# A fused attention, expert and readout kernel: softplus in two chains, and the one-hot rows of the slots placed later in the first expert

## The chip, the cores and the metric

The kernel runs on one core of a Trainium2 chip. The metric is the device time of one launch in microseconds (us). The kernel before was timed three times: 517.79, 516.14 and 516.80 us, median 516.8 us.

## The reference

Three layers follow each other: a retention attention, a layer of 8 experts of which each token uses two, and a dense layer with a softmax-weighted unit and a layer norm.

```
for t in range(S):                                    # B=2, H=8, S=768, D=64
    state = gamma * state + k[:, :, t] (x) v[:, :, t]
    y[:, :, t] = scale * q[:, :, t] @ state
x = y as 1536 rows of 512
logits = x @ w_gate                                   # 512 x 8
noisy  = logits + log1p(exp(x @ w_noise)) * noise
top2 of each row, weights by softmax over the two
out[row] += weight * (relu(x[row] @ w1[e]) @ w2[e])   # w1 512x1024, w2 1024x512, 8 experts
h = out @ w_in; solu = h * softmax(h); ln = (solu - mean) / sqrt(var + 1e-6) * g_ln
result = ln @ w_out
```

## The kernel before, in words

**Stages.** The attention runs over 12 tiles of 128 rows (`for i in range(NT)`): scores, output, state update and a turn of the output into rows (`x_rows`), which also yields the logits of the gate and of the noise scale. The rows are stored to the DRAM tensor `xd`. While it runs, the routing is worked out in four groups of tiles (`GROUPS`: tiles 0 to 3, 4 to 7, 8 and 9, 10 and 11). Then eight experts are worked through, one after the other, and after them the dense layer, again by tiles of 128 rows.

**Number format.** The experts' matmuls take each operand as a high and a low part (`wh` and `wl` of the weights, `xh` and `xl` of the rows, `hh` and `hl` of the hidden values). ACT writes the high part as a copy, DVE the low part as a difference. A hidden group (`hidden(e, f, ...)`, line 723) is 12 matmuls into one PSUM bank: eight with `xh`, then four with `xl`. ACT (line 727) and DVE (line 728) empty it.

**Routing.** `choose(g)` computes the softplus of the noise scale with a polynomial of degree 8 in |tanh(z/2)| (line 509, seven dependent steps), the noisy logits, the top two (`top`, `chosen`) and a running count (`cum`). `rank(g)` turns `chosen` and `cum` into ranks with two small matmuls. `slots(lo, hi)` works in two halves: first the ranks of the two chosen experts of every row (lines 564 to 571), then one-hot rows `nm` and `hot` (lines 579 to 585). `add_table` multiplies `nm` with `hot` on PE and adds the result to `table`, which then tells which row stands in which slot. `by_rows` spreads it, `lists` makes from it the row numbers `rows_r` for experts 1 to 7 (line 671), and `load_xg(1)` gathers the 448 rows of expert 1 from `xd` with four indirect DMAs on POOL (line 998). Those rows are turned by PE (line 1028) inside the second half of expert 0 (`second`, line 1071).

**Expert 0 is split.** Which rows it has is known in two steps: 192 early rows from tiles 0 to 7 (`first_xt(0, ...)`) and 256 late rows (`list_part(1, ...)`, gathered and turned by `first_xt(1, ...)`, lines 634 to 639). The loop at line 971 runs the eight hidden groups f = 0 to 7 for the early rows; the loop at line 1087 runs the same eight for the late rows. Between the groups stand the routing steps, at places written out by hand with conditions on f. Everything is issued in the order in which the Python code runs (a manual schedule): each engine takes its own instructions in that order, so a step on DVE delays all that is written after it on DVE.

**Weights.** `advance(0, j)` after every second late group splits one more weight unit (lines 200 and 201) and issues later loads.

Of the kernel before, what the change touches and what calls it, by code (L numbers as in the profile page):

```python
# [8 lines left out]
F32 = mybir.dt.float32  # L9
# [6 lines left out]
AF = mybir.ActivationFunctionType  # L16
OP = mybir.AluOpType
# [5 lines left out]
LOG2 = (0.006006605044301197, -0.034264599930674204, 0.09229041734241328, -0.16499812980379158,  # L23
        0.2394333707327323, -0.331446652240305, 0.49982549864312487, -0.999993630258501,
        0.6931471414508898)
# [19 lines left out]
def retnet_moe_solu(ctx, tc, qT, kT, k, v, w_gate, w_noise, noise, w1, w2, w_in, w_out, g_ln,  # L45
                    decay, out, dbg=None):
    nc = tc.nc
# [4 lines left out]
    E = w1.shape[0]  # L52
# [229 lines left out]
    causal = const.tile([128, 128], F32, name="causal")  # L282
# [3 lines left out]

    decT = {}
    step = const.tile([128, NC, HP], F32, name="step")
    one = rt.tile([1, 128], F32, name="one", bufs=1)
    nc.gpsimd.memset(one, 1.0)  # L290

    def dec_t(c):
        if c >= NC:
# [197 lines left out]
    def choose(g):  # L491

        lo, hi = GROUPS[g]
        n_t = hi - lo
        t = rt.tile([128, 4, n_t, E], F32, tag="rt", name="rt", bufs=3)
        th, r, ab, nl = (t[:, n] for n in range(4))
        p = lgs[:, lo:hi]
        ii = slice(lo, hi)
        V = nc.vector

        nc.scalar.activation(th, p[:, :, E:2 * E], AF.Tanh, scale=0.5)
        nc.scalar.activation(r, p[:, :, E:2 * E], AF.Relu)
        yield
        V.scalar_tensor_tensor(ab, th, -1.0, th, op0=OP.mult, op1=OP.max)
        V.tensor_scalar_mul(nl, ab, LOG2[0])
        for n, c in enumerate(LOG2[1:-1]):
            if n == 2 and g == 2:
                yield
            V.scalar_tensor_tensor(nl, nl, c, ab, op0=OP.add, op1=OP.mult)
        V.scalar_tensor_tensor(nl, nl, LOG2[-1], r, op0=OP.add, op1=OP.add)  # L510
        V.tensor_mul(nl, nl, nz[:, ii, :])
        V.tensor_add(nl, nl, p[:, :, :E])
        yield
        ix = rt.tile([128, n_t, 8], U32, tag="ix", name="ix")
        for s in range(n_t):
            V.max(top[:, lo + s, :], nl[:, s])
        V.tensor_tensor(chosen[:, ii, :], nl, top[:, ii, 1:2].to_broadcast([128, n_t, E]), op=OP.is_ge)
        for i in range(lo, hi):
            V.tensor_add(cum[:, i + 1], cum[:, i], chosen[:, i])
        yield  # L520
        for s in range(n_t):
            V.max_index(ix[:, s], top[:, lo + s, :], nl[:, s])
        V.tensor_copy(top_i[:, ii, :], ix[:, :, :2])
# [447 lines left out]
    for f in range(KF):  # L971
        hidden(0, f, slice(0, EARLY), (lambda: newest(2 + f // 2)) if f in (0, 2) else None)
        if f == 3:
            list_part(1, range(4, 12), "c2", last=True)
            for p in last_picks:
                next(p, None)
            todo = slots(4, 10)
            next(todo)
        if f == 4:
            turns()  # L980
        if f == 5:
            next(todo, None)
            next(picks, None)
    for p in range(2):
        first_xt(1, 2 * p)

# [96 lines left out]
    for e in range(E - 1):  # L1083
        if e:
            hidden_of(e)
        for j in range(4):
            for f in (2 * j, 2 * j + 1):
                hidden(e, f, slice(0 if e else EARLY, CAPS[e]))
                if not e and f == 0:
                    todo = slots(10, NT)  # L1090
                    next(todo)
                if not e and f == 1:
                    next(todo, None)
                if not e and f == 3:
                    add_table(4, "c2")
                    add_table(10, "c3")
                    by_rows()
                if not e and f == 5:
                    lists()
                    for _ in load_xg(1):  # L1100
                        pass
                    rt_ctx.close()
                    gx["pool"] = gx_ctx.enter_context(tc.tile_pool(name="gx", bufs=1, side="right"))
                if e == 1 and f in (1, 3):
                    next(rows, None)
                if e and e + 2 < E and f < 4:
                    fresh = fresh if f else load_xg(e + 2)
                    nc.gpsimd.tensor_copy(pace, H_t[e][0][:1, f, :1])  # L1108
                    next(fresh)
                if e and f in (5, 7):  # L1110
                    next(fresh, None)
                if e and f in (1, 3, 4, 5):
                    d = (1, 3, 4, 5).index(f)
                    y_st = y_t(e - 1, d)
                    next(y_st, None)
                    y_bank(e, d)
                elif e:
                    convert()
                    if f == 6:
                        next(y_st, None)  # L1120
                elif not e and f > 5:
                    for d in ((0, 1), (2, 3))[f - 6]:
                        y_bank(e, d)
            advance(e, j)
            if e and j > 1:
                next(y_st, None)
# [259 lines left out]
```

## Time and profile before

| | |
|---|---|
| median of three runs | 516.8 us |
| the profiled execution: its time | 515.93 us |
| its span on the core | 513.8 us |
| PE busy | 505.3 us (98%) |
| DVE busy | 365.7 us (71%) |
| ACT, POOL busy | 232.2 us (45%), 111.2 us (22%) |
| late rows' first hidden group starts | 82.21 us |
| second half of expert 0 starts | 96.64 us |

Times of the trace are counted from the start of the span. PE is the matmul engine and PEld its weight loads; a busy PE is not a PE at its peak, since matmuls overlap and their ends are modelled. A row of the timeline has the start, the duration, the engine, the line, the operation with output and inputs, and in brackets the idle time of the engine just before it with what ended it.

### The profile page before, as it was taken

To read this page: it belongs to the slowest core of one execution; us is meant where nothing else is said; L and a number is where in the kernel's file an instruction comes from. 1 tells how busy PE (TensorE), PEld (TensorE's weight loads), DVE (VectorE), ACT (ScalarE), POOL (GpSimd) and SP (SyncE) were. 2 spreads that over 40 slices of the span, in tenths; PEclk is the share of its full clock that TensorE was granted. 3 is DMA by queue.
4 is the path that set the end of the run, shared out by engine and by line. 5 is a ranking of instruction groups with operands and counts; after the bars stand their busy time and mean duration, and the time that the engine had idled before them with its cause. 6 is when DMAs were issued, how large, how long until landed. Compare 5 with 4: busy or idle time off the path is not lost.

```text
span 513.8 us, 8621 instructions
## 1 busy us (share of the span) xinstructions
PE 505.3 (98%) x3068; PEld 462.7 (90%) x3068; DVE 365.7 (71%) x726; ACT 232.2 (45%) x436; POOL 111.2 (22%) x210
## 2 busy tenths in 40 slices
PE   9999998999999999999999999999999999999996
PEld 8898987999999999999999999998878788888885
DVE  5678778846876886787869778799187657676650
ACT  2488733643353443345335534445244634345431
POOL 4034100423003104004003000002344435431120
PEclk9999999999999999999999999999999999999999
DMA  8999531798989898989799968567553564653341
GB/s 256 308 390 355 196 99 43 236 363 250 311 251 243 283 265 214 347 214 279 262 277 305 304 169 264 183 179 202 173 175 122 145 186 141 174 160 122 102 124 47
DMA packets 71857, 111.92 MB, mean 218 GB/s; under 512 B 9760, under 2 KB 37152, under 8 KB 71808
## 3 DMA queue, kind: packets, MB, share of 16 engines
q1 hardware_dynamic: 65952, 96.54, 61.5%
q0 software_dynamic: 4368, 14.29, 9.1%
q10 hardware_dynamic: 1488, 0.48, 0.4%
q8 instruction: 26, 0.43, 0.3%
q14 instruction: 23, 0.19, 0.1%
HBM read 83.50 MB, written 27.79 MB: 217 GB/s over the span
## 4 chain that ended last, share of the span: by engine, by line
PE 80%; DVE 12%; ACT 2%; issue 2%; DMA 2%; SPq 0%; DVEq 0%; ACTq 0%
PE c L1071 21%; PE b L952 11%; PE a L723 10%; PE b L723 10%; PE d L859 10%; PE c L1193 3%; PE xr L479 3%; PE s L429 3%; PE c L446 2%; PE c L457 2%; PE c L442 2%; DVE wl L201 1%; DVE hl L728 1%; DVE yr L1052 1%; PE a L837 1%
## 5 line engine op out<-in xcount | busy, mean ns | idle before, releaser
L201 DVE TENSOR_TENSOR wl<-wr,wh 128x1024 fp32r<-128x1024 f32 x64 | 76.6, 1219 | 12.4 <-ACT wh L200 12.4
L1071 PE MATMUL c<-hh,wh 128*128 128x448 f32 (+5 forms) x224 | 79.0, 352 | 0.0
L1071 PE MATMUL c<-hh,wl 128*128 128x448 f32 (+5 forms) x224 | 78.8, 352 | 0.0
L1071 PE MATMUL c<-hl,wh 128*128 128x448 f32 (+5 forms) x224 | 78.8, 352 | 0.0
L200 ACT ACTIVATE wh<-wr 128x1024 fp32r<-128x1024 f32 x68 | 69.4, 1050 | 7.1 <-DMA wr<-in_moe_w_dram 7.0
L723 PE MATMUL b<-xh,wh 128*128 128x192 f32 (+8 forms) x144 | 47.1, 335 | 0.3 <-ACT xh L638 0.3
L723 PE MATMUL b<-xh,wl 128*128 128x192 f32 (+8 forms) x144 | 46.6, 331 | 0.0
L1071 PEld LDWEIGHTS c<-hh,wl 128*128 128x128 f32 x224 | 42.1, 188 | 1.1
L1071 PEld LDWEIGHTS c<-hl,wh 128*128 128x128 f32 x224 | 42.1, 188 | 1.1
L1071 PEld LDWEIGHTS c<-hh,wh 128*128 128x128 f32 x224 | 42.1, 188 | 1.1
L723 PE MATMUL a<-xh,wh 128*128 128x256 f32 (+7 forms) x128 | 42.9, 340 | 0.0
L723 PE MATMUL a<-xh,wl 128*128 128x256 f32 (+7 forms) x128 | 42.8, 339 | 0.0
L859 PE MATMUL d<-wh,x2h 128*128 128x512 f32 x96 | 38.8, 404 | 0.0
L1108 POOL COPY pace<-hh 1x1 f32<-1x1 f32 x20 | 9.8, 490 | 133.0 <-ACT hh L727 133.0
L952 PE MATMUL b<-wh,zh 128*128 128x512 f32 (+1 forms) x104 | 38.3, 375 | 0.0
L952 PE MATMUL b<-wl,zh 128*128 128x512 f32 (+1 forms) x104 | 38.3, 374 | 0.0
L859 PE MATMUL d<-wl,x2h 128*128 128x512 f32 x96 | 37.9, 395 | 0.0
L859 PE MATMUL d<-wh,x2l 128*128 128x512 f32 x96 | 37.8, 394 | 0.0
L727 ACT ACTIVATE hh<-b 128x192 fp32r<-128x192 f32 (+8 forms) x36 | 17.1, 476 | 44.0 <-PE b L723 42.2
L727 ACT ACTIVATE hh<-a 128x256 fp32r<-128x256 f32 (+7 forms) x32 | 15.9, 497 | 45.3 <-PE a L723 45.3
L998 POOL DMA_INDIRECT xr<-xd,rows_r x27 | 28.3, 1048 | 26.2 <-DVE rows_r L671 16.8
L1034 ACT ACTIVATE xh<-xt 128x428 fp32r<-128x428 f32 (+5 forms) x24 | 13.0, 542 | 44.8 <-DVE xt L1032 44.8
(254 smaller groups left out, 1093.4 us busy)
## 6 DMA issues: line engine op xcount, KB each, us to landing
wr<-in_moe_w_dram SPq DMA_DIRECT2D x64, 512.0 KB, 5.5
zd<-zs SPq DMA_DIRECT2D x40, 128.0 KB, 2.3
zc<-zd SPq DMA_DIRECT2D x10, 512.0 KB, 4.0
xs<-xr SPq DMA_DIRECT2D x18, 256.0 KB, 5.6
raw<-in_moe_w_in_dram SPq DMA_DIRECT2D x8, 512.0 KB, 6.4
raw<-in_moe_w_out_dram SPq DMA_DIRECT2D x8, 512.0 KB, 5.9
xq<-xs SPq DMA_DIRECT2D x16, 208.0 KB, 7.1
yg<-yr SPq DMA_DIRECT2D x16, 208.0 KB, 4.7
```

The costliest lines, as they stand in the source:

```text
L200: nc.scalar.activation(hi, t, AF.Copy)
L201: (nc.gpsimd if u < LEAD else nc.vector).tensor_sub(lo, t, hi)
L429: nc.tensor.matmul(p[:, s, hp, :], KT[i][r, hp, :], QT[i][r, hp, :], start=True, stop=True)
L479: nc.tensor.matmul(t[:, d // 2, at:at + 128 + G2], XT[i][:, d, :], unit[d // 2][:, G2 - G2 * (d % 2):][:, :128 + G2], start=(d % 2 == 0), ...
L723: nc.tensor.matmul(p, w[:, 0, f * 128:(f + 1) * 128], x[:, d, c], start=(n == 0), stop=(n == len(terms) - 1))
L727: nc.scalar.activation(hh[:, f, c], p, AF.Relu)
L859: nc.tensor.matmul(PH[i][:, s, :], x[:, c], w[:, 0, f], start=(n == 0), stop=(n == 3 * KD - 1))
L952: nc.tensor.matmul(p, z[:, f * 128:(f + 1) * 128], unit_t[8 * E + 4 + f // 2][n][:, f % 2, c], start=(m == 0), stop=(m == len(terms) - 1))
L998: nc.gpsimd.indirect_dma_start(out=t[b], out_offset=None, in_=xd[:], in_offset=bass.IndirectOffsetOnAxis(ap=rows_r[:, e - 1, b:b + 1], axi ...
L1034: nc.scalar.activation(hi, t, AF.Copy)
L1071: nc.tensor.matmul(py[d][:, :CAPS[e]], c, h[:, f, :CAPS[e]], start=(f == 0 and n == 0), stop=(f == KF - 1 and n == 2))
L1193: nc.tensor.matmul(py, h[:, f, c], w[:, f % 2], start=(f == 0 and n == 0), stop=(f == KF - 1 and n == 2))
```

## The change

Three edits are made.

1. `one`, a row of ones with a memset on POOL, is now the first row of `causal`.
2. In `choose`, ACT also computes the square of the tanh (`sq`), and the polynomial is worked out as two chains in `sq`, one for the even and one for the odd powers, which are added at the end.
3. The second half of `slots(4, 10)` and the last step of `choose(3)` leave the early loop. They stand after late groups 1 and 0. `slots(10, 12)` moves from late groups 0 and 1 to 2 and 3, the tables from 3 to 4, `lists` and the gathers of expert 1 from 5 to 6.

```diff
-    one = rt.tile([1, 128], F32, name="one", bufs=1)
-    nc.gpsimd.memset(one, 1.0)
+    one = causal[0:1, :]
...
-        t = rt.tile([128, 4, n_t, E], F32, tag="rt", name="rt", bufs=3)
-        th, r, ab, nl = (t[:, n] for n in range(4))
+        t = rt.tile([128, 5, n_t, E], F32, tag="rt", name="rt", bufs=3)
+        th, r, ab, nl, sq = (t[:, n] for n in range(5))
+        od = th
...
         nc.scalar.activation(th, p[:, :, E:2 * E], AF.Tanh, scale=0.5)
+        nc.scalar.activation(sq, th, AF.Square)
         nc.scalar.activation(r, p[:, :, E:2 * E], AF.Relu)
         yield
         V.scalar_tensor_tensor(ab, th, -1.0, th, op0=OP.mult, op1=OP.max)
-        V.tensor_scalar_mul(nl, ab, LOG2[0])
-        for n, c in enumerate(LOG2[1:-1]):
+        V.tensor_scalar_mul(nl, sq, LOG2[0])
+        V.tensor_scalar_mul(od, sq, LOG2[1])
+        for n in (2, 4, 6):
+            V.scalar_tensor_tensor(nl, nl, LOG2[n], sq, op0=OP.add, op1=OP.mult)
+            V.scalar_tensor_tensor(od, od, LOG2[n + 1], ab if n == 6 else sq, op0=OP.add, op1=OP.mult)
             if n == 2 and g == 2:
                 yield
-            V.scalar_tensor_tensor(nl, nl, c, ab, op0=OP.add, op1=OP.mult)
         V.scalar_tensor_tensor(nl, nl, LOG2[-1], r, op0=OP.add, op1=OP.add)
+        V.tensor_add(nl, nl, od)
...
         if f == 4:
             turns()
-        if f == 5:
-            next(todo, None)
-            next(picks, None)
...
                 if not e and f == 0:
+                    next(picks, None)
+                if not e and f == 1:
+                    next(todo, None)
+                if not e and f == 2:
                     todo = slots(10, NT)
                     next(todo)
-                if not e and f == 1:
+                if not e and f == 3:
                     next(todo, None)
-                if not e and f == 3:
+                if not e and f == 4:
                     add_table(4, "c2")
                     add_table(10, "c3")
                     by_rows()
-                if not e and f == 5:
+                if not e and f == 6:
                     lists()
```

**On DVE, in the softplus of the last group** (tile `rt` holds all its operands; `nz` is the noise, `lgs` the logits). Before:

```order
L504 SCALAR_TENSOR_TENSOR rt<-rt 128x16
L505 TENSOR_SCALAR rt<-rt 128x16
L509 SCALAR_TENSOR_TENSOR rt<-rt 128x16 x7
L510 SCALAR_TENSOR_TENSOR rt<-rt 128x16
L511 TENSOR_TENSOR rt<-rt,nz 128x16
L512 TENSOR_TENSOR rt<-rt,lgs 128x16
```

With the change:

```order
L506 TENSOR_SCALAR rt<-rt 128x16
L507 TENSOR_SCALAR rt<-rt 128x16
L509 SCALAR_TENSOR_TENSOR rt<-rt 128x16
L510 SCALAR_TENSOR_TENSOR rt<-rt 128x16
L509 SCALAR_TENSOR_TENSOR rt<-rt 128x16
L510 SCALAR_TENSOR_TENSOR rt<-rt 128x16
L509 SCALAR_TENSOR_TENSOR rt<-rt 128x16
L510 SCALAR_TENSOR_TENSOR rt<-rt 128x16
L513 SCALAR_TENSOR_TENSOR rt<-rt 128x16
L514 TENSOR_TENSOR rt<-rt 128x16
L515 TENSOR_TENSOR rt<-rt,nz 128x16
L516 TENSOR_TENSOR rt<-rt,lgs 128x16
```

The instructions of lines 509 and 510 belong to two chains in turn, and no instruction of one needs the one just ahead of it.

**On DVE, from the last early groups to the first late ones** (`nm` and `hot` the one-hot rows, `xl` the late rows' low parts, `hl` the hidden values' low parts, `wl` a weight unit's). Before:

```order
L728 SCALAR_TENSOR_TENSOR hl<-c_1359,hh 128x192
L579 TENSOR_TENSOR nm<-col_185,at 128x384
L582 TENSOR_TENSOR nm<-nm,number 128x384
L585 TENSOR_TENSOR hot<-col_185,at 128x1536
L522 MAX_INDEX ix<-top,rt 128x8 x2
L523 CAST top_i<-ix 128x4
L728 SCALAR_TENSOR_TENSOR hl<-b,hh 128x192
L728 SCALAR_TENSOR_TENSOR hl<-c_1397,hh 128x192
L639 TENSOR_TENSOR xl<-a,xh 128x2x256 x2
L728 SCALAR_TENSOR_TENSOR hl<-b,hh 128x256
L564 TENSOR_TENSOR eq<-e_180,top_i 128x32
```

With the change:

```order
L643 TENSOR_TENSOR xl<-a,xh 128x2x256 x2
L732 SCALAR_TENSOR_TENSOR hl<-b,hh 128x256
L526 MAX_INDEX ix<-top,rt 128x8 x2
L527 CAST top_i<-ix 128x4
L732 SCALAR_TENSOR_TENSOR hl<-a,hh 128x256
L583 TENSOR_TENSOR nm<-col_183,at 128x384
L586 TENSOR_TENSOR nm<-nm,number 128x384
L589 TENSOR_TENSOR hot<-col_183,at 128x1536
L201 TENSOR_TENSOR wl<-wr,wh 128x1024
L732 SCALAR_TENSOR_TENSOR hl<-b,hh 128x256
L568 TENSOR_TENSOR eq<-e_178,top_i 128x32
L569 TENSOR_TENSOR eq<-eq,rks 128x32
```

The six instructions of the one-hot rows and of the top-two numbers now stand behind `xl`, and the first weight unit's `wl` stands ahead of the last group's `eq`, not behind its `hot`.

**On DVE, to the row numbers of the later experts** (`spread` is the table by rows, `rows_r` the row numbers). Before:

```order
L600 TENSOR_TENSOR spread<-part_211,table 128x128
L201 TENSOR_TENSOR wl<-wr,wh 128x1024
L728 SCALAR_TENSOR_TENSOR hl<-b,hh 128x256
L728 SCALAR_TENSOR_TENSOR hl<-a,hh 128x256
L671 TENSOR_SCALAR rows_r<-c_1572 128x28
```

With the change:

```order
L604 TENSOR_TENSOR spread<-part_209,table 128x128
L732 SCALAR_TENSOR_TENSOR hl<-a,hh 128x256
L201 TENSOR_TENSOR wl<-wr,wh 128x1024
L732 SCALAR_TENSOR_TENSOR hl<-b,hh 128x256
L675 TENSOR_SCALAR rows_r<-c_1599 128x28
```

`rows_r` now follows the `hl` of late group 6, before it followed that of group 5.

## Rows read from the trace of the kernel before

**Rows 1.** The page's first part: busy time, share of the span, instructions.
```profile
PE 505.3 (98%) x3068; PEld 462.7 (90%) x3068; DVE 365.7 (71%) x726; ACT 232.2 (45%) x436; POOL 111.2 (22%) x210
```

**Rows 2.** Waits of PE, whole run: us in total, times, longest.
```profile
PE b L723 <- DVE xl L639: 1.5, 1, 1.5
```

**Rows 3.** Timeline of DVE: dependent steps of the softplus, then two independent ones.
```profile
70.18 1.43 DVE L509 SCALAR_TENSOR_TENSOR rt<-rt 128x16 f32<-128x16 f32 x7
...
78.16 0.17 DVE L570 SCALAR_TENSOR_TENSOR at<-top_i,sets 128x12 f32<-128x12 f32 x1
78.25 0.17 DVE L571 SCALAR_TENSOR_TENSOR at<-sets,ranks 128x12 f32<-128x12 int32 x1
```

**Rows 4.** Timeline of PE: first matmuls of early groups 1, 2 and 3.
```profile
69.66 0.33 PE L723 MATMUL c<-xh,wh 128*128 128x192 f32 x1
...
71.06 0.27 PE L723 MATMUL b<-xh,wh 128*128 128x192 f32 x1
...
73.14 0.33 PE L723 MATMUL c<-xh,wh 128*128 128x192 f32 x1
```

**Rows 5.** Timeline of PE's weight loads: the output of attention tile 11.
```profile
65.05 0.45 PEld L446 LDWEIGHTS c<-pm,vp 128*64 128x64 f32 x8 [0.20 <-ACT lg L484]
```

**Rows 6.** Timeline of DVE, around the late rows' low parts.
```profile
80.45 0.55 DVE L579 TENSOR_TENSOR nm<-col,at 128x384 f16<-128x384 f32 x1
...
83.17 0.08 DVE L522 MATCH_VALUE_LOAD ix<-top,rt 128x8 f32 x1
...
84.19 1.28 DVE L639 TENSOR_TENSOR xl<-a,xh 128x512 fp32r<-128x512 f32 x2
...
86.82 0.18 DVE L564 TENSOR_TENSOR eq<-e,top_i 128x32 f32<-128x32 f32 x1
...
87.91 0.42 DVE L728 SCALAR_TENSOR_TENSOR hl<-a,hh 128x256 fp32r<-128x256 f32 x1
88.25 0.28 DVE L579 TENSOR_TENSOR nm<-col,at 128x128 f16<-128x128 f32 x1
...
89.38 1.22 DVE L201 TENSOR_TENSOR wl<-wr,wh 128x1024 fp32r<-128x1024 f32 x1
90.51 0.42 DVE L728 SCALAR_TENSOR_TENSOR hl<-b,hh 128x256 fp32r<-128x256 f32 x1
```

**Rows 7.** Timeline of PE: first matmuls of late groups 0, 1, 2 and 5.
```profile
82.21 0.39 PE L723 MATMUL b<-xh,wh 128*128 128x256 f32 x1 [0.25 <-ACT xh L638]
...
85.86 0.28 PE L723 MATMUL a<-xh,wh 128*128 128x256 f32 x1
...
87.29 0.28 PE L723 MATMUL b<-xh,wh 128*128 128x256 f32 x1
...
92.10 0.28 PE L723 MATMUL a<-xh,wh 128*128 128x256 f32 x1
```

**Rows 8.** Timeline of ACT: a weight unit's high part.
```profile
94.02 1.05 ACT L200 ACTIVATE wh<-wr 128x1024 fp32r<-128x1024 f32 x1
```

**Rows 9.** Timeline of DVE: the row numbers and that unit's low part.
```profile
94.50 0.18 DVE L671 TENSOR_SCALAR rows_r<-c 128x28 uint32<-128x28 f32 x1
95.11 1.23 DVE L201 TENSOR_TENSOR wl<-wr,wh 128x1024 fp32r<-128x1024 f32 x1 [0.43 <-ACT wh L200]
```

**Rows 10.** Timeline of POOL: the fourth gather for expert 1.
```profile
98.71 1.54 POOL L998 DMA_INDIRECT xr<-xd,rows_r  x1 [0.31 <-issue]
```

**Rows 11.** Line 998, the fourth gather alone: from its start to its landing.
```profile
DMA to landing us min/median/max: 7.8/7.8/7.8
```

**Rows 12.** Line 998 from 90 to 135 us, all twelve gathers.
```profile
DMA to landing us min/median/max: 3.4/7.0/8.9
```

**Rows 13.** Timeline of PE's weight loads: expert 1's rows turned, eight blocks.
```profile
106.17 1.00 PEld L1028 LDWEIGHTS a<-unit,xr 128*128 128x128 f32 x8
```

**Rows 14.** Timeline of PE: the last matmuls of the launch.
```profile
508.27 1.07 PE L952 MATMUL b<-wh,zl 128*128 128x256 f32 x8
```

**Rows 15.** Windows: busy us and count of PE, PEld, DVE, ACT, POOL; granted clock, DMA, GB/s.
```profile
512.00:513.80 1.80, 0.00 (x0) 0.00 (x0) 0.00 (x0) 0.00 (x0) 0.00 (x0) 0.95 0.04 9
```

## The prediction

> **What bounds the kernel now.** I read the page's first part first. PE is busy for 98% of the span [rows 1], so a change can only take away, add or move waits of PE. The waits come next: over the whole run PE's longest wait for another engine is one of 1.5 us, for `xl`, the late rows' low parts, which DVE writes [rows 2]. Then come the timelines of PE and DVE from 60 to 107 us, the stretch that the change touches. There PE loses time in three places.
>
> First, the output of attention tile 11: its weight loads waited 0.20 us [rows 5]. The row names ACT, but what comes last there is DVE's masked scores, which stand behind the third group's softplus in DVE's order. Second, the last group's softplus: early group 1 of expert 0 took 71.06 - 69.66 = 1.40 us, early group 2 took 73.14 - 71.06 = 2.08 us, since `rank` behind it waits for `chosen`; 0.68 us are lost [rows 4]. Third, late group 0: it took 85.86 - 82.21 = 3.65 us where group 1 took 1.43 us [rows 7]. DVE was busy with one-hot rows from 80.45 to 83.17 us and came to `xl` only at 84.19 us [rows 6]. That loses 2.22 us. Together some 3.1 us can be won here. From 106 us on PE hardly waits, so what is won or lost up to there reaches the end.
>
> **The change, part by part.** The row of ones in place of a memset on POOL costs and gives nothing: POOL's first work lies under the loads of the start. Four more squares on ACT cost PE nothing either, because ACT is busy 45% of the span [rows 1]; were that cover gone, four instructions of some 0.2 us would be 0.8 us. No table is loaded more often in the changed order.
>
> *Two chains.* Before, 11 steps from the first product to the noisy logits depend on each other, 1.43 / 7 = 0.20 us apart. Two steps that don't depend on each other start 0.09 us apart (78.16 and 78.25) [rows 3]. With two chains the longer one has 8 steps, and the other's fit between them. That is 3 x 0.20 = 0.6 us less for the last group, nearly all of the 0.68 us that PE loses. Of the third group's second half two steps go, 0.4 us, more than the 0.20 us [rows 5]. I take 0.83 us for both places together.
>
> The Trainium skill has a rule that speaks against this part: on VectorE: DVE Perf Modes, section "The DRAIN you can't avoid", says that the next instruction doesn't start until the pipe is empty, so that independent instructions gain nothing. By it the 13 instructions in place of 12 would cost 0.2 us, not save 0.6. The pair of rows 3 speaks against it here, so I go by the pair.
>
> *`xl` first.* The one-hot rows (80.45 to 83.17, 2.72 us) and the top-two numbers leave the place ahead of `xl` [rows 6]. DVE is then free when ACT has written `xh`, and the `xl` matmuls start almost without a wait; I leave 0.1 us for that and win 2.1 us. Late group 1 would start at 85.86 - 0.83 - 2.1 = 82.93 us, group 2 at 84.36 us [rows 7].
>
> *What is late next.* The removed work now stands behind `xl` on the same engine, and PE meets it at the tables, four groups later. `hl` of group 1 starts 87.91 - 87.29 = 0.62 us behind group 2's first matmul [rows 6, 7], so at 84.98 us. From there DVE has no idle time up to the last one-hot rows: `hl` 0.34 (87.91 to 88.25), the big one-hot rows 2.72, a weight unit's `wl` 90.51 - 89.38 = 1.13, `hl` 0.34, the ranks from `eq` on 87.91 - 86.82 = 1.09, `hl` 0.34, the small one-hot rows 89.38 - 88.25 = 1.13 [rows 6]. The sum is 7.09 us, and they are written at 92.07 us. PE has finished groups 1 to 4 at 82.93 + 4 x 1.43 = 88.65 us and the larger table about 0.3 us later. It waits some 3.1 us. Group 5 then starts at about 92.25 us, against 92.10 us before [rows 7]. The wait for `xl` has become a longer wait one place later, and the balance is +0.15 us. Small errors in the seven durations and the two gains make this -0.4 to +0.6 us.
>
> *Row numbers for expert 1.* They move behind group 6, and on DVE behind its `hl` and a weight unit. ACT's split of that unit started 94.02 - 92.10 = 1.92 us after group 5 [rows 7, 8]; now 94.17 us. Its `wl` starts 95.11 - 94.02 = 1.09 us later [rows 8, 9], at 95.26, and ends at 96.39 us; `hl` takes 0.34 us more. `rows_r` starts at 96.75 us, where it was 94.50 us [rows 9]: 2.25 us later. Behind it waits POOL with the four gathers. The fourth started at 98.71 us [rows 10] and landed 7.8 us later [rows 11], at 106.51 us. PE's weight loads for the first eight turned blocks run from 106.17 us, 0.125 us apart, and the fourth block comes at 106.55 us [rows 13]. There is no slack: 0.04 us. With the change the gather starts at 100.96 us and PE asks for it at 106.70 us.
>
> How long it then takes isn't shown before, since the weight loads that share the DMA engines stay where they are. From below: 5.7 us or less hides it, and the shortest of the twelve gathers took 3.4 us. From above: 8.9 us, the longest, makes PE wait 109.86 - 106.70 = 3.15 us [rows 12]. I take the median, 7.0 us [rows 12], because this gather falls among the same loads as those that took about that long: landing at 107.96 us, a wait of 1.25 us. Nothing behind it gives that back.
>
> **Sum.** +0.15 + 1.25 = +1.4 us on the profiled execution of 515.93 us, so 517.3 us. That execution lies 0.9 us under the median of the three runs; on the median the forecast is 516.8 + 1.4 = 518.2 us. A measurement of this kernel can tell about 0.3% from no change, 1.55 us, so this counts as no change.
>
> **Rivals.**
> - *A, the forecast:* gains and the new wait for the one-hot rows cancel, and the gather lands 5.7 to 7.15 us after its start: 0 to 1.4 us of wait, time up to 518.35 us. With it the case of a hidden gather: 516.95 us. 0.52.
> - *B, slower:* the gather decides. From 7.15 us on the sum is over 1.55 us; at 8.9 us it is 0.15 + 3.15 = 3.3 us, 520.1 us. For it: the fourth gather took 7.8 us [rows 11], and would meet all of its competitors from the start. Against it: with a later start less of its own queue lies ahead of it, and the loads are further on. 0.30.
> - *C, slower, the clock:* PE stands still for 3.1 us at the tables, longer than anywhere between its first matmul and its last. After its last matmul, over at 509.34 us [rows 14], the granted clock was still nearly full: 0.95 as a mean of the last 1.8 us [rows 15], so it fell to 1.2 GHz only some 4 us after the stop. If it falls earlier here, groups 5 to 7 run at half rate: up to 3 x 1.43 = 4.3 us more, which covers the wait for the gather. With half of that, +0.15 + 2.15 = 2.3 us, 519.1 us. 0.08. The Trainium skill, TensorE: Matmul & The Clock Gate, section "HAM oscillation — how this bites in real kernels", warns of just such waits; by it the fall would come here if the wait grew a little, and no row before shows one in mid run.
> - *D, the chains bring nothing* (each DVE instruction waits for the one ahead of it): the early 0.83 us stay lost, and the one-hot rows and row numbers come 0.8 us later still, so 0.15 + 0.83 + 2.05 = 3.0 us, 519.8 us. Rows 3 speak against it. 0.04.
> - *E, faster:* DVE reaches the last one-hot rows before PE needs them, and the gather is hidden: -2.9 us, 513.9 us. DVE would have to be 3.1 us shorter on seven durations that I read from the trace. 0.06.
>
> **How the numbers follow.** The likeliest case is A: 518.2 us. The chances: faster 0.06 (E), same 0.52 (A), slower 0.42 (B, C, D). The range goes from the hidden gather less the small terms, 516.8 + 0.15 - 0.55 = 516.4 us, to just under the longest gather, 519.9 us; it leaves out E and the ends of B, C and D, less than 2 in 10.
>
> **What would show it.** Right: `xl` at about 82 us with no long wait of PE for it; `chosen` without a wait; the longest wait of PE some 3 us, at line 596, for `hot` on DVE; group 5 within half a microsecond of 92.1 us; `rows_r` near 96.7 us; a wait of PE at the turned rows near 107 us, for a DMA. Wrong: no wait at line 596 (E), a granted clock below 1.00 between 92 and 97 us (C), the steps of lines 509 and 510 spaced 0.2 us apart (D), or PE through the turned rows without a wait, in which case the time stays within half a microsecond of before.

## The result, and the profile after

The changed kernel takes 522.39 us, the median of five executions (520.20 to 523.32); the kernel before, run beside it, took 516.8 us (515.72 to 517.79). The ratio is 1.0104, with an interval of 1.0072 to 1.0136: slower by 5.6 us. The forecast was 518.2 us, and the time lies above its range (516.4 to 519.9).

The profiled execution took 521.80 us (span 519.8 us, mean granted clock 0.995) where before's took 515.93 (513.8, 1.000). Over the five executions the mean clock was 0.990 to 0.995, so all five lost some of it; only the profiled one shows where. The page's first part, against [rows 1]:

```profile
PE 506.6 (97%) x3068; PEld 464.3 (89%) x3068; DVE 365.2 (70%) x730; ACT 233.4 (45%) x440; POOL 108.9 (21%) x209
```

The engines have the same work. The two longest waits of PE over the whole run stand against the one of 1.5 us in [rows 2]:

```profile
PE a L1029 <- DMA xr<-xd,rows_r: 3.3, 2, 1.8
PE c L596 <- DVE hot L589: 3.0, 1, 3.0
```

The wait for `xl` is gone. In its place stand the tables' wait, as forecast, and two waits for gathers that have not landed (lines moved by 1 to 4). How far behind PE runs, from its first matmul of each stage:

| first matmul of | before | after | behind by |
|---|---|---|---|
| late group 0 | 82.21 | 81.65 | -0.56 |
| late group 1 | 85.86 | 83.31 | -2.55 |
| late group 5 (behind the tables) | 92.10 | 92.62 | +0.52 |
| expert 0's second part | 96.64 | 97.22 | +0.58 |
| the same, behind the first turned rows | 107.16 | 111.50 | +4.34 |
| expert 1 | 117.94 | 123.81 | +5.87 |
| end of the span | 513.8 | 519.8 | +6.0 |

So most of the loss arises in two stretches: 3.76 us at the turned rows and 1.53 us right behind them. PE's timeline there, answering to [rows 13]:

```profile
106.96 0.38 PE L1029 MATMUL a<-unit,xr 128*128 128x128 f32 x2
109.12 0.33 PE L1029 MATMUL a<-unit,xr 128*128 128x128 f32 x1 [1.79 <-DMA xr<-xd,rows_r]
110.97 0.86 PE L1029 MATMUL a<-unit,xr 128*128 128x128 f32 x5 [1.52 <-DMA xr<-xd,rows_r]
111.50 0.72 PE L1072 MATMUL c<-hh,wh 128*128 128x448 f32 x1
112.01 0.57 PE L1072 MATMUL c<-hl,wh 128*128 128x448 f32 x1
```

The third gather is waited for, then the fourth. The matmuls behind them run at half rate, as the windows show (columns as in [rows 15]):

```profile
106.00:111.40 5.40, 2.09 (x13) 1.53 (x12) 0.22 (x1) 0.06 (x1) 2.93 (x3) 1.00 1.03 377
111.40:114.60 3.20, 3.20 (x12) 2.88 (x10) 2.65 (x6) 1.96 (x3) 0.00 (x0) 0.52 1.05 404
114.60:118.00 3.40, 3.40 (x17) 3.09 (x16) 1.00 (x1) 0.00 (x0) 0.00 (x0) 0.95 0.63 152
```

After 3.3 us of standing still the granted clock is 0.52 for 3.2 us, nearly all at 1.2 GHz: 3.20 x 0.48 = 1.5 us, and 3.40 x 0.05 = 0.2 us after it, together about what the table shows for this stretch. POOL's timeline shows why the gathers are late, against [rows 10]; DVE's row of the same stretch stands under it:

```profile
97.62 0.94 POOL L999 DMA_INDIRECT xr<-xd,rows_r  x1 [20.07 <-DVE rows_r L675]
98.87 1.97 POOL L999 DMA_INDIRECT xr<-xd,rows_r  x1 [0.30 <-issue]
101.14 1.96 POOL L999 DMA_INDIRECT xr<-xd,rows_r  x1 [0.30 <-issue]
103.40 0.95 POOL L999 DMA_INDIRECT xr<-xd,rows_r  x1 [0.30 <-issue]
...
98.79 4.63 DVE L201 TENSOR_TENSOR wl<-wr,wh 128x1024 fp32r<-128x1024 f32 x4 [0.52 <-ACT wh L200]
```

The second and third gather take twice as long as the first. In the kernel before, the gathers began at 94.95 us, and three of them, of 0.95 us each, had begun when DVE's four `wl` began at 98.20 us. Now `rows_r` comes 2.67 us later, but the four `wl`, tied to ACT's splits, come only 0.59 us later (98.79), and the gathers fall among them. The fourth starts 4.69 us later than before, not 2.25. From its start to its landing it takes about as long as before (7.8 us in [rows 11]), so it lands late because it starts late:

```profile
DMA to landing us min/median/max: 7.5/7.5/7.5
```

### The profile page after: what moved, and what is told of

Same layout as the page of the kernel before. It is cut to its first block, busy times and chain, and to the rows that moved or that the text cites. A ratio compares the mean times of both kernels' runs of the same rounds, so it can differ in the third digit from the quotient of the medians.

```text
span 519.8 us, 8624 instructions
## 1 busy us (share of the span) xinstructions
PE 506.6 (97%) x3068; PEld 464.3 (89%) x3068; DVE 365.2 (70%) x730; ACT 233.4 (45%) x440; POOL 108.9 (21%) x209
## 4 chain that ended last, share of the span: by engine, by line
PE 78%; DVE 7%; issue 7%; DMA 3%; ACT 2%; POOL 1%; SPq 0%; DVEq 0%; POOLq 0%; ACTq 0%
PE c L1072 20%; PE b L956 11%; PE a L727 10%; PE b L727 10%; PE d L863 10%; PE c L1198 3%; PE xr L478 3%; PE s L428 3%; PE c L445 2%; PE c L456 2%; PE c L441 2%; DMA xr<-xd,rows_r 1%; DVE wl L201 1%; PE a L841 1%; PE c L269 1%
```

## The experiments

**1. The chains alone.** The kernel before with the new `choose` and the shared row of ones, all moves left out:

```diff
-        V.tensor_scalar_mul(nl, ab, LOG2[0])
...
+        for n in (2, 4, 6):
+            V.scalar_tensor_tensor(nl, nl, LOG2[n], sq, op0=OP.add, op1=OP.mult)
+            V.scalar_tensor_tensor(od, od, LOG2[n + 1], ab if n == 6 else sq, op0=OP.add, op1=OP.mult)
```

> The kernel before with the two chains and the row of ones alone; no instruction changes its place. My theory (what costs is the place of the row numbers for expert 1, not the chains): PE's wait for the last group's chosen goes, late group 1 starts 0.5 to 0.7 us earlier, and the time is 0.3 to 0.7 us under before (516.1 to 516.5 us). Rival (each DVE instruction waits for the one ahead of it): no gain or 0.2 us slower, and the steps of the two chains stand 0.2 us apart.

Measured: 516.62 us against 517.27, ratio 0.9994 (0.9972 to 1.0016): no change. In its trace POOL's four gathers start 0.46 us earlier than before, and PE doesn't wait for `chosen`; so the chains save about that much where they stand, just under what was expected. PE still waits 1.5 us for `xl`. A gain of 0.1% can't be told from none.

**2. The moves alone.** The kernel before with all moves made, and with its own `choose` and row of ones:

```diff
-        if f == 5:
-            next(todo, None)
-            next(picks, None)
...
                 if not e and f == 0:
+                    next(picks, None)
+                if not e and f == 1:
+                    next(todo, None)
+                if not e and f == 2:
                     todo = slots(10, NT)
                     next(todo)
...
-                if not e and f == 5:
+                if not e and f == 6:
                     lists()
```

> The change without the two chains: the polynomial in one chain, all moves made. My theory: the loss is the moves' alone, so PE waits about 3 us at the tables, the fourth gather starts later still by some 0.5 us, PE waits for it 4 us or more, the granted clock falls behind that wait, and the time is 522 to 524 us. Rival (the chains cost something, by the four squares on ACT or the longer list of DVE instructions): under 521 us.

Measured: 522.05 us, ratio 1.0088 (1.0059 to 1.0117). The moves make the loss. PE waits 3.0 us for `hot` and 2.4 us for the gathers, not the 4 us or more that were expected: the clock fell behind the tables as well (0.74 from 92 to 98 us), so PE came later. Behind the gathers it fell again (0.58 from 111.4 to 114.6 us).

**3. Lists and gathers one group earlier**, behind group 5 as before:

```diff
-                if not e and f == 6:
+                if not e and f == 5:
                     lists()
```

> The change with the row numbers and the gathers for expert 1 back behind late group 5 (the tables stay behind group 4). My theory (the loss comes from the late gathers and the clock that falls behind PE's wait for them): row numbers about 2 us earlier, at 95.1 us, the fourth gather starts by 100 us and lands by 108 us, PE waits for it under 1 us, the granted clock stays 1.00, and the time is 517 to 518.5 us. Rival (the 3 us wait at the tables is what lowers the clock or costs the time): still 521 us or more, with a clock below 1.00.

Measured: 518.95 us, ratio 1.0043 (1.002 to 1.0066). The gathers start at 95.82, 97.07, 98.33 and 99.58 us, all take 0.95 us, and PE doesn't wait for them. By the ratios 3.2 us of the 5.4 are gone. But 2.2 us stay, the time is above the 518.5 us that were the most expected, and the trace has a fall of the clock that the change's own trace had not, behind the tables (the second row is the change's):

```profile
92.00:98.00 6.00, 5.77 (x38) 5.65 (x39) 4.20 (x10) 1.71 (x3) 1.88 (x2) 0.72 0.41 118
...
92.00:98.00 6.00, 5.49 (x46) 5.46 (x47) 4.73 (x11) 2.29 (x5) 0.38 (x1) 1.00 0.49 134
```

6.00 x 0.28 = 1.7 us. Up to the tables the two kernels are the same, with the same wait of 3.0 us, so the fall differs from execution to execution.

**4. The rows turned later.** Expert 1's rows are turned one step later in expert 0's second part, and the gathers stay late:

```diff
-            for d in ((0, 1), (2, 3), (), ())[j] if e else ((), (0, 1), (2, 3), ())[j]:
+            for d in ((0, 1), (2, 3), (), ())[j] if e else ((), (), (0, 1), (2, 3))[j]:
```

> The change with the turning of expert 1's rows moved one step later in the second half of expert 0 (behind its third and fourth quarter): the gathers keep their place, PE asks for them 4.9 us later. My theory: the wait for the gathers goes, the granted clock stays 1.00; a new wait of 1 to 2 us comes at the first hidden group of expert 1, for its low parts; 518 to 519.5 us. Rival (the clock falls for the wait at the tables): clock below 1.00 and 520 us or more.

Measured: 518.62 us, ratio 1.0044 (1.0023 to 1.0065). There is no wait at the turned rows, though the fourth gather starts as late as 102.15 us. The new wait expected at expert 1 didn't come either; again the clock falls behind the tables instead (0.72 from 92 to 98 us in the profiled execution), so the time lies in the expected range by luck. Runs 3 and 4 remove the wait for the gathers in opposite ways and land within 0.35 us of each other: by their times that wait is worth 3 to 4 us, net of a fall of the clock that came at the tables instead.

**5. No `wl` beside the gathers.** Units 8 to 11 are split behind the turned rows:

```diff
-        up = 8 * e + (AHEAD[j] if e or j > 3 else 5 + j)
+        up = 8 * e + (AHEAD[j] if e or j > 4 else (5, 6, 7, 8, 8)[j])
```

> The changed kernel, with the splits of the weight units 8 to 11 (the four `wl` of 4.63 us that run from 98.79 beside the gathers) issued behind the turn of expert 1's first rows instead of ahead of it. Theory (DVE's `wl` slows POOL's gather instructions from 0.95 to 1.97 us, and so the fourth starts 4.7 us later): with no `wl` beside them all four take 0.95 us, the fourth starts at 101.4 to 102.4, lands near 108.9, the wait of TensorE at L1029 shrinks from 7.1 us in all to under 2.5, and the time comes to 518 to 519.5. Rival (the gathers wait for the DMA queues, whatever DVE does): their instructions still take 1.9 us, the fourth starts after 103, the wait stays over 5 us, the time over 520. A third possibility is that the weights split later are missed by TensorE in expert 1 (a wait for `wl` or `wh` at L727 at 112 or later), which would hide a gain: then the starts of the gathers tell.

Measured: 517.7 us against 517.4, ratio 1.0003 (0.9985 to 1.0021): the whole loss is gone, more than was expected. POOL's timeline, and the one `wl` that is left there, that of unit 7:

```profile
97.81 0.95 POOL L999 DMA_INDIRECT xr<-xd,rows_r  x1 [20.11 <-DVE rows_r L675]
99.06 1.96 POOL L999 DMA_INDIRECT xr<-xd,rows_r  x1 [0.30 <-issue]
101.33 0.95 POOL L999 DMA_INDIRECT xr<-xd,rows_r  x1 [0.30 <-issue]
102.58 0.95 POOL L999 DMA_INDIRECT xr<-xd,rows_r  x1 [0.30 <-issue]
...
98.98 1.23 DVE L201 TENSOR_TENSOR wl<-wr,wh 128x1024 fp32r<-128x1024 f32 x1 [0.52 <-ACT wh L200]
```

Only the gather that meets this `wl` takes 1.96 us. The fourth still starts at 102.58, though, 0.8 us earlier than in the change: most of the help comes from its landing, 4.1 us after its start where the change took 7.5:

```profile
DMA to landing us min/median/max: 4.1/4.1/4.1
```

The later splits also hold back the weight loads that they let go (the load that left at 100.23 us landed at 104.21, and the next left at 112.08 us), so this run takes away two things at once. The tables' wait of 3.0 us stayed, and with it alone PE is 0.78 us behind before at the second part and still at expert 1, near the change's 0.58 us at the second part.

**6. Splits behind the lists.** Lists behind group 5, and weight units 4 to 6 split behind them:

```diff
-        up = 8 * e + (AHEAD[j] if e or j > 3 else 5 + j)
+        up = 8 * e + (AHEAD[j] if e or j > 3 else (4, 4, 6, 8)[j])
...
-                if not e and f == 6:
+                if not e and f == 5:
```

> The changed kernel with the lists and gathers behind group 5, and with the splits of the weight units 4, 5 and 6 issued behind the lists, so that no `wl` of 1.22 us stands ahead of the slots' one-hot rows or the tables' sums on DVE. Theory: `hot` of slots 10 ends one `wl` earlier (91.3), the tables' wait falls from 3.0 to about 1.9 us, no longer enough for the granted clock to fall (it did not behind before's 1.5 us wait), the gathers start by 93.5 to 94.5 at 0.95 us each and land before they are wanted; the second part of expert 0 starts at 96.1 (before 96.6), and the time comes to 516 to 517, no slower than before. Rival (the clock falls behind a wait of 1.9 us as well, or units 4 to 6 come too late for the second part, which then waits for `wh` or `wl` at L1072): 518 to 519.

Measured: 519.06 us, ratio 1.0041 (1.0021 to 1.0062): the rival. The tables' wait fell to 1.9 us as expected, yet the clock fell behind it:

```profile
92.00:98.00 6.00, 6.00 (x39) 6.00 (x39) 3.05 (x7) 2.55 (x4) 1.86 (x2) 0.72 0.09 18
```

The gathers start at 95.83 us, not by 94.5. And the later splits let the loads of units 8 to 11 go later: DVE stands 4.62 us, waiting for unit 11, with `xl` of expert 1 behind it, for which PE then waits 0.9 us.

```profile
112.73 1.23 DVE L201 TENSOR_TENSOR wl<-wr,wh 128x1024 fp32r<-128x1024 f32 x1 [4.62 <-ACT wh L200]
113.88 1.15 DVE L1036 TENSOR_TENSOR xl<-a,xh 128x448 fp32r<-128x448 f32 x2
```

**7. The last tiles' slots first.** As run 6, and the ranks and one-hot rows of tiles 10 and 11 go ahead of those of tiles 4 to 9:

```diff
                 if not e and f == 0:
                     next(picks, None)
+                    late = slots(10, NT)
+                    next(late)
                 if not e and f == 1:
-                    next(todo, None)
+                    next(late, None)
                 if not e and f == 2:
-                    todo = slots(10, NT)
-                    next(todo)
-                if not e and f == 3:
                     next(todo, None)
```

> As the previous one, and the slots of the last two tiles are done ahead of those of tiles 4 to 9: `picks`, ranks and positions of slots 10 behind group 0 of the late rows, their one-hot rows behind group 1, the large one-hot rows of slots 4 behind group 2. DVE's idle stretches of 1.0 us at 82.9 and 0.5 us at 85.0 then hold work. Theory: `hot` ends near 89.5 instead of 92.4, TensorE waits under 1 us for the tables, no clock falls, the second part of expert 0 starts at 94 to 94.5 (before 96.6), the gathers are issued from 92.5 on and land by 104; if TensorE does not wait there, the time comes to 514 to 515, faster than before and than the change. Rival (what PE no longer waits for at the tables it waits for later: gathers that have not landed when expert 1's rows are turned 2.4 us earlier, or weights 4 to 7 split too late): the start of expert 1's first part stays near 107 and the time within 1 us of before's 516.8.

Measured: 519.24 us, ratio 1.003 (1.0011 to 1.0049): in kind the rival, though PE waits neither for gathers nor for weights 4 to 7. The tables' wait is 1.3 us, above the 1 us expected, and the second part starts at 95.56 us, 1.1 us ahead of before. But unit 11 still blocks `xl` (its `wl` starts at 111.80 us), PE, which comes earlier than in run 6, waits 2.4 us there, and the granted clock is 0.61 in the 3.4 us from 114.6 us on. The lead becomes a wait at the next queue, and the wait costs clock.

**8. `wl` in halves.** The changed kernel, with `wl` of units 7 to 11 written by two instructions of half the size:

```diff
-            (nc.gpsimd if u < LEAD else nc.vector).tensor_sub(lo, t, hi)
+            if 7 <= u <= 11:
+                for h in range(2):
+                    c = (slice(0, 1), slice(h * 512, h * 512 + 512)) if j < 4 else (slice(h, h + 1), slice(0, 512))
+                    nc.vector.tensor_sub(lo[:, c[0], c[1]], t[:, c[0], c[1]], hi[:, c[0], c[1]])
+            else:
+                (nc.gpsimd if u < LEAD else nc.vector).tensor_sub(lo, t, hi)
```

> The changed kernel, with DVE's `wl` of weight units 7 to 11 done in two instructions of half the size (about 0.65 us each instead of 1.22). Theory, from the starts and ends in the runs so far: a gather instruction that starts while a `wl` runs waits for the end of that one instruction and then takes 0.91 us, so its length is the rest of the `wl` plus 0.91. With half-size `wl` no gather of expert 1 takes more than 1.6 us, the second and third take 1.1 to 1.6 instead of 1.97 and 1.96, and the fourth starts 4.2 to 4.6 us after the first instead of 5.78. Rival (the two engines share the way to the memory in proportion, as long as any `wl` runs): the second and third keep 1.9 to 2.0 us and the fourth starts 5.6 us or more behind the first.

Measured, one execution: 520.51 us. POOL, and DVE under it:

```profile
98.22 0.94 POOL L1004 DMA_INDIRECT xr<-xd,rows_r  x1 [20.96 <-DVE rows_r L680]
99.47 0.94 POOL L1004 DMA_INDIRECT xr<-xd,rows_r  x1 [0.30 <-issue]
100.71 1.43 POOL L1004 DMA_INDIRECT xr<-xd,rows_r  x1 [0.30 <-issue]
102.44 0.95 POOL L1004 DMA_INDIRECT xr<-xd,rows_r  x1 [0.30 <-issue]
...
100.03 4.99 DVE L204 TENSOR_TENSOR wl<-wr,wh 128x512 fp32r<-128x512 f32 x8 [0.52 <-ACT wh L200]
```

The halves end 0.60 us apart: 100.72, 101.32, 101.92, 102.53. The gather of 100.71 starts in the second, which ends at 101.32, and is over at 102.14, 0.82 us later. The one of 102.44 starts 0.09 us ahead of an end, in the middle of the row of eight, and takes 0.95 us. If the two engines shared in proportion, it would have taken 1.9. The fourth starts 4.22 us behind the first instead of 5.78. The theory holds. PE waits 1.6 us instead of 3.3, but only in part for this: in this execution the clock fell behind the tables as well (0.72 from 92 to 98 us), and PE comes to the turned rows 1.24 us later.

**9. Slots ahead of everything.** The order of run 7, moved one step further ahead, with splits that keep the loads early and units 8 to 11 behind the turned rows:

```diff
-        up = 8 * e + (AHEAD[j] if e or j > 3 else 5 + j)
+        up = 8 * e + (AHEAD[j] if e or j > 4 else (4, 5, 7, 8, 8)[j])
...
-                hidden(e, f, slice(0 if e else EARLY, CAPS[e]))
                 if not e and f == 0:
                     next(picks, None)
+                    late = slots(10, NT)
+                    next(late)
                 if not e and f == 1:
-                    next(todo, None)
-                if not e and f == 2:
-                    todo = slots(10, NT)
-                    next(todo)
-                if not e and f == 3:
+                    next(late, None)
+                hidden(e, f, slice(0 if e else EARLY, CAPS[e]))
+                if not e and f == 1:
                     next(todo, None)
...
-                if not e and f == 6:
+                if not e and f == 5:
```

> The changed kernel with the slots of the last two tiles ahead of all else: `picks`, ranks and positions right behind `xl` (DVE idles there for 1.0 us), their one-hot rows ahead of group 1, the large ones of tiles 4 to 9 behind group 1; lists and gathers behind group 5; weight units 4, 5 and 6, 7 split behind groups 3, 5 and 7, units 8 to 11 behind the turn of expert 1's rows. Theory: `hot` ends near 89.2, TensorE waits under 0.3 us for the tables, the clock has no cause to fall, the second part of expert 0 starts at 93.5 to 94.3 (before 96.6), the gathers start at 92.7 to 93.2. If expert 1's rows are there when TensorE turns them at 103.4, the time is 514 to 515; if they land at 105 to 106 as they do before, TensorE waits 1.5 to 2.5 us there and the gain is nearly all given back: 516 to 517. Rival (the early weight loads that the earlier splits let go still crowd the gathers or `xl`, as in the previous run with moved splits): 518 or more.

Measured: 516.35 us against 516.75, ratio 0.9981 (0.996 to 1.0002): at the edge of what can be told. The tables' wait is gone, 0.7 us are lost for `spread` and 0.5 us for the gathers, and no fall of the clock is left in its trace. The second part starts at 95.23 us, later than expected. One of its twelve executions took 1009.98 us at a mean granted clock of 1.000; the ratio leaves it out, and no trace shows what happened in it.

**10. The same, with the rows turned later**, as in run 4.

> The same with expert 1's rows turned one step later in expert 0's second part (as in the run of that change alone), so that the gathers have 4.5 us more. Theory: no wait for the gathers; the second part's lead of 2.4 to 3 us over before is kept to the end and the time comes to 513.5 to 515, under before and under the previous run by its wait. Rival (expert 1's first group then waits for `xh`, `xl` or for its weights, split behind the turn and so later too): the start of expert 1's first part is no earlier than before's and the time 516 or more.

Measured: 515.59 us, ratio 0.997 (0.9953 to 0.9987): faster than before and than the change, by less than expected. PE's waits from 78 to 125 us, all of them:

```profile
PE c L673 <- DVE spread L604: 0.7, 1, 0.7
PE b L727 <- ACT xh L642: 0.2, 1, 0.2
```

The second part starts at 94.97 us, 1.67 us ahead of before, and expert 1 at 116.09 us, 1.85 us ahead, but the span is only 0.4 us shorter than that of before's profiled execution. The lead goes in experts 1 and 2: their four halves start 1.85, 1.38, 1.00 and 0.74 us ahead, expert 3 0.49 us, and little is lost after it. PE waits for nothing in this stretch and the granted clock is 1.00, but expert 1's matmuls start 0.207 us apart where before's start 0.203 us apart. Run 9's trace has the same spacing there; why is not shown. What run 10 gains is steadiness: its twelve executions took 515.04 to 516.09 us at mean granted clocks of 0.998 to 1.000, where before's beside them took 515.38 to 519.61 us, at clocks of 0.995 to 1.000.

**11. The loads held back.** The changed kernel with the splits of units 7 to 11 in place, but the loads of units 12 to 15 behind the first two stores of expert 2's rows:

```diff
-        feed(up, up + 3)
+        feed(*((12, 12) if not e and 4 <= j < 7 else (up, up + 3)))
```

> The changed kernel with the splits of weight units 7 to 11 where they are, but the loads that these splits let go, of units 12 to 15, issued behind the first two stores of expert 2's rows instead of beside expert 1's gathers. It keeps what delays the gathers' start on POOL and takes away what shares the DMA engines with them; the previous run with halved `wl` did the opposite, and the run with the later splits did both. From `rows_r` to the landing of the fourth gather it takes 12.0 us before, 13.7 with the change, 12.5 with halved `wl`, 9.3 with later splits. Theory (both count: the start by about 1.2 us, the sharing by about 3): the second and third gather still take 1.97 us on POOL, the fourth starts 5.8 us behind the first, but lands 4 to 5.5 us after its start instead of 7.5, so 10.2 to 11.7 us behind `rows_r`; TensorE waits 0.5 to 2 us at L1029 and the time is 518 to 520. Rival (the landing is late for the late start alone): 7 us or more to the landing, 13 us or more behind `rows_r`, a wait over 3 us and a time over 520.5.

Measured: 520.77 us, ratio 1.0071 (1.0051 to 1.0091). The third and fourth gather started at 102.69 and 104.52 us (1.52 and 1.96 us on POOL) and landed 7.5 and 7.9 us after their start. Holding these loads did not shorten the landing, so that half of the theory fell. The rival's numbers are met at the landing and in the time, just missed from `rows_r` to the landing (99.74 to 112.44 us, 12.7) and not in PE's wait (1.7 us; PE itself came later, after a fall of the clock to 0.53 from 92 to 98 us). Unit 11's load and one of `raw` still left SP at 103.42 and 103.86 us and landed at 110.50 and 111.93, beside these gathers, so sharing isn't excluded either: in run 5 no load was under way from 104.21 us to the landing. What made run 5's landing 4.1 us stays open.

## Why the prediction was wrong

**Right.** The two chains' steps start 0.10 us apart; `chosen` is not waited for; early group 2 takes 1.58 us instead of 2.08. `xl` starts at 81.62 us. The tables' wait is 3.0 us (forecast 3.1), group 5 starts at 92.62 (92.25), `rows_r` at 97.17 us (96.75). The gains were a little smaller than forecast: 0.56 us for the chains (0.83), 1.99 us for `xl` (2.1). DVE's timeline of the chains, against [rows 3]:

```profile
70.29 0.18 DVE L509 SCALAR_TENSOR_TENSOR rt<-rt 128x16 f32<-128x16 f32 x1
70.39 0.17 DVE L510 SCALAR_TENSOR_TENSOR rt<-rt 128x16 f32<-128x16 f32 x1
70.50 0.17 DVE L509 SCALAR_TENSOR_TENSOR rt<-rt 128x16 f32<-128x16 f32 x1
```

The Trainium skill's section that the prediction set against the chains (VectorE: DVE Perf Modes, "The DRAIN you can't avoid") also says that a next instruction that isn't held (made to wait until all earlier ones have finished) starts earlier. The trace agrees with that part: these steps take 0.17 us each and start 0.10 us apart.

Up to the second part the balance was +0.58 us, where +0.15 with an upper end of +0.6 was forecast.

**The step that failed** is the last term: "With the change the gather starts at 100.96 us", and with it the wait of 1.25 us. It moved the fourth gather by the 2.25 us of `rows_r` and took POOL's three gathers ahead of it at their old 0.95 us. The measured start is 103.40 us: 0.42 us since `rows_r` itself came later than forecast, 1.02 + 1.01 us for the second and third gather's waits behind `wl`. The landing took 7.5 us where the median of 7.0 was taken. So the start was off by 2.44 us and the landing by 0.5, and the stage lost 3.76 us instead of 1.25. The sum also put the clock behind this wait at nothing, where it cost 1.53 us. With what was measured the terms are 0.58 + 3.76 + 1.53 = 5.87 us, where 0.15 + 1.25 was forecast. The prediction named the queue behind `rows_r` and didn't ask what DVE does beside it; its own rows held the sign, for the fourth gather of before took 1.54 us [rows 10].

Runs 5 and 8 show the cause of the late start: whether a gather takes 0.95 or up to 1.97 us depends on whether a `wl` runs when it starts. Run 2 shows that the moves bring the loss in, runs 3 and 4 that the larger part of it is the wait for the gathers. What sets the time from a gather's start to its landing stays open.

**The rivals.** B, the gather decides, was the right direction: its price ended at 3.15 us of wait and 520.1 us. C, the clock, was priced as a case of its own, at the tables. In the profiled execution the clock stayed full there and fell behind the gathers, after B's wait, for 1.5 us; in the traces of runs 2, 3, 4, 6, 8 and 11 it did fall behind the tables, for 1.5 to 2.5 us. The two are not alternatives: in this trace the fall came behind B's wait. B's bound with half of C's loss, 0.15 + 3.15 + 2.15 = 5.45 us, would have given 522.3 us, near the measured time partly by luck, since none of the three terms is the measured one. The falls also came behind waits shorter than the 3.1 us at which the prediction gave C its small chance: 1.9 us in run 6, 2.4 us in run 7. D is excluded by the rows above and by the 0.46 us of run 1; E by the wait at line 596.

## What to carry to other kernels

When a queue of gathers on POOL is moved, lay DVE's timeline beside it: what costs is not how much DVE does but whether a long instruction of the wrong kind is running at the moment when each gather starts. A wait that is moved to another place is not priced by its length alone when PE stands still for 2 to 3 us: add the clock behind it as part of the same case. And before work is put off to a place where "the engine has room", follow what its end releases (buffers, loads, the next instruction on its queue): runs 6 and 7 won at the tables and lost it at unit 11 and to the clock.

## What the runs showed of the hardware that was not expected

A gather instruction that starts while `wl` runs (two inputs and one output in SBUF) waits for the end of that one instruction, and is over 0.8 to 0.9 us after it; one that starts outside takes 0.95 us. In the kernel before, the first gather and then the POOL and DVE rows behind [rows 10] follow; the four `wl` end about 1.14 us apart, at 99.42, 100.56, 101.70 and 102.83 us:

```profile
94.95 0.95 POOL L998 DMA_INDIRECT xr<-xd,rows_r  x1 [16.81 <-DVE rows_r L671]
...
100.55 1.97 POOL L998 DMA_INDIRECT xr<-xd,rows_r  x1 [0.30 <-issue]
102.82 0.95 POOL L998 DMA_INDIRECT xr<-xd,rows_r  x1 [0.30 <-issue]
...
98.20 4.63 DVE L201 TENSOR_TENSOR wl<-wr,wh 128x1024 fp32r<-128x1024 f32 x4 [0.52 <-ACT wh L200]
```

The gather of [rows 10] ends at 100.25 us, these two at 102.52 and 103.77 us: 0.8 to 0.9 us behind the first, third and fourth `wl`. `hl`, which reads one of its inputs from PSUM, doesn't do this: before's third gather started at 97.45 us while an `hl` ran (97.25 to 97.68) and took 0.95 us. ACT's split alone doesn't either: in run 7 a gather beside `wh` (100.79 to 101.85 us), with DVE idle, took 0.95 us from 100.72 on. The Trainium skill, SBUF — State Buffer, section "SBUF: two separate sides", has a rule for it: a DVE instruction with two SBUF inputs and a GpSimd instruction that reads SBUF (this gather reads `rows_r`) contend for a shared pair of ports, which the one that starts first keeps for its whole instruction, and the other is blocked instead of sharing. The traces agree for a gather that comes second, by the ends above and by run 8. They don't show the other direction: before's `wl` of 95.11 us [rows 9] starts inside the first gather, and takes 1.23 us like the others.

The clock is the second thing. Behind waits of PE of 1.9 to 3.3 us the granted clock fell for some 3 us or more in some executions (0.52 behind the gathers; 0.53 to 0.74 as a mean over 92 to 98 us in runs 2, 3, 4, 6, 8 and 11) and not in others (1.00 behind the tables in the change's own profile and in run 5, after the same 3.0 us). From the last matmul of the tables to the second part PE took 4.6 us where the clock stayed at 1.00 (the change, run 5), 6.1 to 6.3 us in runs 2, 3, 4, 6 and 8, and 7.15 us in run 11: a fall cost 1.5 to 1.6 us, in run 11 2.5. Runs 9 and 10, in whose traces PE never waits more than 0.8 us there, keep mean clocks of 0.998 and more in every execution. That the spread of the kernel before comes from its wait of 1.5 us for `xl` fits this, but no trace here shows where its clock fell.
